# The dense activations' turned copies made in the forward chain instead of between the chains

## The chip, the cores and the metric

The kernel runs on one core of a Trainium2 chip. The metric is the device time of one execution in microseconds. A core has five engines with a queue of instructions each, executed in order: TensorE (PE) for matmuls, VectorE (DVE), ScalarE (ACT), GpSimd (POOL), and SyncE (SP), which here only issues transfers. Transfers run on 16 DMA engines that all queues share. PE reads its operands from on-chip memory (SBUF) and writes to accumulators (PSUM); the inputs, outputs and larger intermediates lie in DRAM.

## The reference

The kernel computes a forward pass and all its gradients. With `xn` the layer norm of `x` (2048 rows of 512), the output is `x + A(xn) + B(xn)`:

```python
# A: 64 segments of 32 rows, 8 memory rows carried from segment to segment
h = concatenate([mem, xs])                     # 40 x 512
q, k, v = h @ Wq, h @ Wk, h @ Wv               # 32 heads of 128
p = softmax(mask(q @ k.T * scale))             # 40 x 40 a head
o = (p @ v) @ Wo
mem, outs[s] = o[:8], o[8:]
# B
a = relu(xn @ w1 + b1) ** 2                    # 2048 x 1792
out = a @ w2 + b2
```

It returns the output and the gradients for `x`, the first memory, `Wq`, `Wk`, `Wv`, `Wo`, `w1`, `b1`, `w2` and `b2`, given `grad_out`, all in bfloat16. Two of them matter here: the gradient of `w2` is `a.T @ grad_out` and that of `w1` is `xn.T @ gh1`, where `gh1` is the gradient at `xn @ w1 + b1`. Both sum over all 2048 rows.

## The kernel before

The work runs in five stages, one after the other on PE. The times are those of the profiled execution.

1. **Dense part B** (0 to some 250 us): four blocks of 512 rows (`RB`). It makes `a` and `gh1` turned, with the 1792 features along the partitions, and stores them as `S_AT[rb]` and `S_GH1T[rb]` in DRAM (1792 x 512 each, rows of 1 KB).
2. **The forward chain** (some 250 to 1140 us): 64 steps, one for each segment, each waiting for the memory rows of the one before. Four steps make a block (`b`), and the memory rows of a whole block are computed apart in "left" work that runs some blocks behind or ahead.
3. **Between the chains** (some 1140 to 1377 us): 16 blocks of the first part of the backward pass for the memory rows (`lback`), and beside it, in the PE slots that `product` fills, the gradients of `w2` and `w1`.
4. **The backward chain** (some 1377 to 2340 us): 64 steps in the other direction.
5. **The weight gradients** of the attention (to the end at 2913 us).

**The order of work** in the stages 2 to 4 is written by hand. `F_ORDER` holds four strings, one for each step of a block; `play` (in the functions below) goes through them and calls each named operation. A plus or a minus behind a name shifts it to a later or an earlier step: `soP++` belongs to the step one before that of the names with three pluses. `L.` marks left work of a block. The calls issue instructions on all engines, and each engine's queue keeps the order of the calls. So the place of a name also decides where its transfer stands in SP's queue.

The names that matter, with the lines of the profile:

- `ld` (`load`, L639) loads 8 memory rows of v for a later step into `f_vLs`, four transfers of 16 KB. `w0` and `w1` read them on PE.
- `soV`, `soN`, `soP` (L956, L957, L958) store v, k with q, and the softmax `E` of a step to `S_A`. `E` is one tile, without a second buffer: the next step's `pm0` (DVE, L607) writes it again once the store has landed.
- `L.t0` to `L.t3` (L758) turn a quarter of a block's attention output by a DMA transpose of 256 KB into `OC`, a single buffer, and `L.u0` to `L.u3` (L766) store it.
- `L.lv` (L746), `L.lm` (L634) load `VL` and the four pieces of `vM`, 64 KB each; `L.W0` and `L.W1` on PE (L620, written as `f_pp<-ETL,vM`) read both.
- `kl` and `km` (L894, L895) are POOL's copies of the memory rows' keys into and out of `f_kT`; `kl` must be done before the step's scores.
- `L.hl`, `L.lq`, `L.ldL`, `L.lb` load further tiles, each well ahead of its use.

A transfer on SP also waits for the transfer eight places ahead of it in the same queue, since SP's transfers share eight semaphores in turn.

**Between the chains** `LB_ORDER` fixes the order of one block. Its `ld` (L1011 to L1014 and L629) loads the next block's `vTL` (a DMA transpose), `vTM`, `P`, `kM` in four pieces and `kL`, and then calls `chunk`. The gradient products go by 256 features at a time (`CH`), 7 for `w2` in the blocks 1 to 7 and 7 for `w1` in the blocks 9 to 15. For each, `chunk` brings one side into `wB` (two buffers of 1 MB, 128 partitions x 16 row blocks x 256 features, so that rows lie along the partitions): four DMA transposes of 256 x 512 on SP (L1085), one for each block of 512 rows. The other side (`wA`: `grad_out`, later `xn`, 2 MB) is loaded once by POOL (L1082). `product` multiplies half a piece at a time, 32 matmuls of 512 columns in a block (L1101, for `w2`) or 64 of 256 (L1106, for `w1`). A block of this stage on PE has in addition the projections by `Wo` (L422), the scores (L467) and the outer products (L620).

Two tiles of 128 KB, `XL0` and `X0`, hold the first left rows and the first block's input. They are made at the end of stage 1; `XL0` is read before the chain, `X0` by the first four steps and by a store to `S_HT`.

Of the kernel before, what the change touches and what calls it, by code (L numbers as in the profile page):

```python
# [10 lines left out]
BF16 = mybir.dt.bfloat16  # L11
F32 = mybir.dt.float32
P = 128
# [13 lines left out]
def kernel(  # L27
# [27 lines left out]
    nc = tc.nc  # L55
# [4 lines left out]
    F = B_w1.shape[1]  # L60
    SEG = int(A_seg_len)
    assert Dh == P and D % P == 0 and F % P == 0 and S % P == 0 and D <= 512
    L = M + SEG
    assert L <= 64 and P % SEG == 0
    NSEG = S // SEG
    DC = D // P
    TC = S // P
# [54 lines left out]
    S_GXNB = dram.tile([S, D], F32, name="S_GXNB")  # L122
    S_AT = dram.tile([NRB, F, RB], BF16, name="S_AT")
    S_GH1T = dram.tile([NRB, F, RB], BF16, name="S_GH1T")

    AC = 3 * GW + KH * KW
    S_A = dram.tile([NSEG, HG, SEG, AC], BF16, name="S_A")
# [526 lines left out]
    def play(order, n, steps, lefts, step, blk, done=None):  # L654
# [18 lines left out]
                            done(k)  # L673


    F_ORDER = (
# [3 lines left out]
        "ta+++ Ha+++ L.u2 L.mx0+ L.t1 soV+++ tb+++ L.X2 Hb+++",  # L680
# [5 lines left out]
        "rb+++ L.oa0+ ta+++ Ha+++ tb+++ Hb+++",  # L686
# [4 lines left out]
        "tu1+++ w1+++ L.lq++ oa1+++ ob1+++ g0+++ g1+++ soN++ ra+++ rb+++ ta+++ Ha+++ tb+++ L.otr+ Hb+++",  # L691
# [4 lines left out]
        "ta+++ Ha+++ rb+++ tb+++ Hb+++ km+++ L.t3+ q0mm++++ L.E5+ k0mm++++ L.ra+ xa+++ k0ev++++ q1mm++++ k1mm++++ "  # L696
        "q0ev++++ k0fl++++ q1ev++++ q0fl++++ k1ev++++ q1fl++++ xb+++ k0Te++++ soV++ kl++++ q1Te++++ k1fl++++ "
        "q0Te++++")
    ENGS = on_engines(
        "L.E1 L.E2 L.E4 L.oa0 L.ob0 k0ev k1ev oa0 ob0 ob1 q1Te q1ev ra rb v0ev v1ev",  # L700
        "L.E0 L.E3 L.E5 L.oa1 L.ob1 L.pm0 L.pm1 L.ra k0Te k1Te oa1 pm0 pm1 q0Te q0ev")
    with psum("fr", 4) as fr, psum("fpp", 1) as fpp, \
# [163 lines left out]
        def fwd(s):  # L866
# [84 lines left out]
            for h in range(2):  # L951
                o["H%s" % "ab"[h]] = lambda h=h: HTf(h)
                o["x%s" % "ab"[h]] = lambda h=h: half_over_groups(B_["XT"][:, 2 * h:2 * h + 2, j, M:SEG], st["T", h],
                                                                  slice(M, SEG))
            rows = S_A[s].rearrange("g r c -> (g r) c")
            o["soV"] = lambda: dma(rows[:, 0:GW], T["N"][:, 0, :])  # L956
            o["soN"] = lambda: dma(rows[:, GW:3 * GW], T["N"][:, 1:3, :].rearrange("p t c -> p (t c)"))  # L957
# [1 line left out]
            return o  # L959

        vLs = {}
        TURNS = [(Wqkv[t], n) for t in (1, 0, 2) for n in range(HD * DC // (8 * P))]
        TURNS_O = [(Wo, n) for n in range(HD * DC // (8 * P))]
        with tc.manual_schedule():
# [24 lines left out]
    with sb("la", 2) as la, sb("ls", 2) as ls, sb("lo", 1) as lo_, sb("wg", 2) as wg, psum("lpp", 1) as lpp, psum("lr", 4) as lr:  # L989
# [9 lines left out]
        def lback(i_):  # L999
            b = SEQ[i_]  # L1000
            shapes = {"vTM": [P, KH, HG, NL], "vTL": [P, KH, HG, NL], "P": [P, KH, KW], "kM": [P, GW], "kL": [P, GW],
                      "gON": [P, GW], "gOT": [P, KH, HG, NL],
                      "gS": [P, KH, KW], "gq": [P, KH, HG, NL]}
            home = {"gON": la, "gS": la, "gOT": lo_, "gq": lo_}
            T = Tiles(lambda n: home.get(n, ls).tile(shapes[n], BF16, name="l_" + n, tag=n, bufs=2))
            ps, st, o = {}, {}, {}

            def load(i1, q=nc.sync):
                T1, b1 = lb[i1][1], SEQ[i1]
                turned_rows(T1["vTL"][:], b1, 2)  # L1010
                q.dma_start(T1["vTM"][:], S_VTM[b1])  # L1011
                q.dma_start(T1["P"][:], S_PL[b1])
                memory_rows(T1["kM"], b1, 2 * GW, q)
                q.dma_start(T1["kL"][:], S_NL[b1][:, 1, :])  # L1014

            def ld():
                if i_ + 1 < NB:
                    load(i_ + 1)
                chunk(i_ + 1)
            o["ld"] = ld  # L1020
            o["first"] = lambda: (load(i_, nc.gpsimd), chunk(i_ + 1))
            for i in range(2):
                for x in range(2):
                    o["W%d%s" % (i, "ab"[x])] = lambda i=i, x=x: product(i_, i, x, ps)
                o["v%d" % i] = lambda i=i: keep(i_, i, ps)
                o["x%d" % i] = lambda i=i: store(i_, i, ps)
            for p in range(2):
                def mm(p=p):
                    ps["o", p] = big("ps_proj")
                    proj(ps["o", p], gol[:, :, b * NL:(b + 1) * NL], turned_columns(Wo), p)  # L1030
                o["o%dmm" % p] = mm
                o["o%dev" % p] = lambda p=p: acp(T["gON"][:, HC[p]], ps["o", p][:])

                def fl_(p=p):
                    ps["t", p] = tr("ps_tr")
                    flip(ps["t", p], T["gON"][:, HC[p]])
                o["o%dfl" % p] = fl_
                o["o%dte" % p] = lambda p=p: (acp, vcp)[p](T["gOT"][:, HALF[p]], kgr(ps["t", p]))

                def S_(p=p):  # L1040
                    ps["s", p] = big("ps_sc")
                    scores(ps["s", p], T["gOT"], ((T["vTM"], NL), (T["vTL"], NL)), p, None)
                o["s%d" % p] = S_
                ds_ops(o, p, KW, lambda p=p: ps["s", p], lambda: T["P"], lambda: T["gS"], lo_)

                def tu(p=p):
                    st[p] = ls.tile([P, 4, 2, 32], BF16, name="l_gST", tag="gST%d" % p)
                    turn(st[p], T["gS"], p)
                o["tu%d" % p] = tu

                def qp(p=p):
                    ps["x", p] = [lpp.tile([P, 2, 512], F32, name="l_pp", tag="pp%d" % x) for x in range(2)]
                    outer(ps["x", p], p, ((32, 32, False, 32, T["kM"], lambda k: st[p][:, k % 4, 0, :]),
                                          (32, 32, False, 32, T["kL"], lambda k: st[p][:, k % 4, 1, :])))
                o["qp%d" % p] = qp
                for x, n in enumerate("ab"):
                    o["qe%s%d" % (n, p)] = lambda p=p, x=x: acp(
                        T["gq"][:, HALF[p], 2 * x:2 * x + 2].rearrange("p k g r -> p g k r"), two_of(ps["x", p], x, 32))

            def so():  # L1060
                pdma(S_GOL[b], T["gON"][:])
                pdma(S_GSL[b], T["gS"][:])
                pdma(S_GQL[b], T["gq"][:])
            o["so"] = so
            return o, T
# [7 lines left out]
            n, second = (b - 1, False) if b <= NCH else (b - NCH - 2, True)  # L1073
            return (n if 0 <= n < NCH else None), second

        def chunk(b):
            n, second = job(b)
            if n is None or b in part:
                return
            if n == 0:  # L1080
                side[second] = wg.tile([P, TC, D], BF16, name="wA", tag="wA", bufs=1)
                pdma(side[second][:], (S_XN[:] if second else gflat).rearrange("(c p) f -> p c f", p=P))  # L1082
            part[b] = wg.tile([P, TC, CH], BF16, name="wB", tag="wB")
            for rb in range(NRB):
                nc.sync.dma_start_transpose(part[b][:, rb * RCB:(rb + 1) * RCB],  # L1085
                                            (S_GH1T if second else S_AT)[rb][n * CH:(n + 1) * CH, :])

        def turns(m):
            for x in range(min(m, len(TURNS))):
# [588 lines left out]
```

## Time and profile before

| | us |
|---|---|
| median of 3 timed runs | 2907.44 |
| their lowest and highest | 2903.41, 2910.01 |
| the profiled execution | 2915.0 |
| its span, first to last instruction | 2913.1 |

| engine | busy us | share | instructions |
|---|---|---|---|
| PE (matmul) | 2702.2 | 93% | 51252 |
| PEld (weight load) | 1450.9 | 50% | 51252 |
| DVE | 1277.8 | 44% | 3754 |
| ACT | 1001.7 | 34% | 2330 |
| POOL | 660.6 | 23% | 1278 |

SP has no busy time in this table, since issuing a transfer is not counted; the order of time of its queue shows how long each issue took. The DMA engines moved 561.50 MB, 193 GB/s over the span; 642177 of the 835429 packets were under 512 B.

How to read the lines: a group names source line, engine, operation, output and inputs, then partitions x elements, count and times. "Idle before" is the time in which that engine did nothing ahead of the group's instructions, with what ended it. A line of stretches gives the window and its length, the busy time of PE, PEld, DVE, ACT and POOL with the number of instructions, the granted TensorE clock as a share of full speed, the busy share of the 16 DMA engines (overlapping packets can bring it above 1), and GB/s. A line of an engine's time order gives start, length, engine, line, operation and how many were merged. Waits are listed as total us, number and longest.

### The profile page before, as it was taken

To read this page: it belongs to the slowest core of one execution; us is meant where nothing else is said; L and a number is where in the kernel's file an instruction comes from. 1 tells how busy PE (TensorE), PEld (TensorE's weight loads), DVE (VectorE), ACT (ScalarE), POOL (GpSimd) and SP (SyncE) were. 2 spreads that over 40 slices of the span, in tenths; PEclk is the share of its full clock that TensorE was granted. 3 is DMA by queue.
4 is the path that set the end of the run, shared out by engine and by line. 5 is a ranking of instruction groups with operands and counts; after the bars stand their busy time and mean duration, and the time that the engine had idled before them with its cause. 6 is when DMAs were issued, how large, how long until landed. Compare 5 with 4: busy or idle time off the path is not lost.

```text
span 2913.1 us, 115280 instructions
## 1 busy us (share of the span) xinstructions
PE 2702.2 (93%) x51252; PEld 1450.9 (50%) x51252; DVE 1277.8 (44%) x3754; ACT 1001.7 (34%) x2330; POOL 660.6 (23%) x1278
## 2 busy tenths in 40 slices
PE   7997999999999887888898999999999999999999
PEld 3444555555555555355454554455555444444444
DVE  4533566666665654343454545454445401100000
ACT  2313444444444445232333333333333301111111
POOL 1000000000000001122333433343334324332221
PEclk9998999999999998998899999999999999999999
DMA  9766477667676668999666687677767799999993
GB/s 250 259 207 164 138 184 189 184 188 182 180 192 166 170 156 201 227 225 213 148 167 164 179 220 173 172 180 211 184 170 181 223 273 224 220 209 237 217 210 71
DMA packets 835429, 561.50 MB, mean 193 GB/s; under 512 B 642177, under 2 KB 727698, under 8 KB 833394
## 3 DMA queue, kind: packets, MB, share of 16 engines
q1 hardware_dynamic: 794018, 431.40, 64.6%
q0 software_dynamic: 40912, 122.73, 14.0%
q8 instruction: 402, 6.59, 0.9%
q14 instruction: 97, 0.79, 0.1%
HBM read 174.47 MB, written 234.11 MB: 140 GB/s over the span
## 4 chain that ended last, share of the span: by engine, by line
PE 42%; DMA 7%; issue 2%; DVE 1%; SPq 1%; POOL 0%; ACT 0%; ACTq 0%; DVEq 0%; POOLq 0%
PE ps_gw L1639 17%; PE ps_gR L490 11%; PE ps_proj L422 3%; PE b_pp L620 3%; PE ps_RL L1251 3%; DMA b_kLs<-S_NL 2%; PE b_T L525 1%; PE ps_tr L164 1%; DMA gn<-S_OL 1%; DMA b_qN<-S_A 1%; PE ps_R L490 1%; DMA S_GM<-b_GN 1%; PE b_pp L1383 1%; PE ps_sc L467 1%; DMA b_GN<-GT 0%
## 5 line engine op out<-in xcount | busy, mean ns | idle before, releaser
L1639 PE MATMUL ps_gw<-gn,HNc 128*128 128x512 bf16 x1920 | 416.8, 379 | 0.0
L1639 PEld LDWEIGHTS <-HNc 128*128 128x128 bf16 x1920 | 187.9, 98 | 223.6
L404 ACT CAST f_N<-ps_proj 128x512 bf16<-128x512 f32 x320 | 183.9, 581 | 199.4 <-PE ps_proj L422 192.6
L1572 ACT CAST wt<-ps_gw 128x512 bf16<-128x512 f32 x128 | 74.0, 588 | 451.3 <-PE ps_gw L1639 412.0
L422 PEld LDWEIGHTS <-X 128*32 128x32 bf16 x6144 | 152.6, 96 | 143.1 <-DVE X L534 21.9
L1555 DVE TENSOR_TENSOR gx<-ps_rows,gb 128x512 f32<-128x512 f32 x16 | 11.1, 692 | 426.4 <-PE ps_rows L1553 426.4
L895 POOL COPY kM<-f_kT 128x256 bf16<-128x256 bf16 x64 | 25.8, 403 | 736.0 <-DVE f_kT L407 562.2
L490 PE MATMUL ps_gR<-Wv,gv 128*32 128x512 bf16 x2048 | 145.0, 404 | 6.9 <-issue 6.9
L1639 PE MATMUL ps_gw<-GOc,gn 128*128 128x512 bf16 x640 | 141.0, 383 | 10.2 <-ACT wt L1572 8.7
L490 PE MATMUL ps_gR<-Wk,gk 128*32 128x512 bf16 (+1 forms) x2048 | 141.1, 387 | 1.3 <-ACT gk L404 0.8
L490 PE MATMUL ps_R<-Wo,OT 128*32 128x256 bf16 x4096 | 135.6, 289 | 1.1 <-DVE OT L407 1.1
L422 PE MATMUL ps_proj<-Wq,X 128*32 128x512 bf16 x2048 | 134.7, 380 | 0.1
L404 ACT CAST gk<-b_pp 128x256 bf16<-128x256 f32 x192 | 70.7, 379 | 184.0 <-PE b_pp L620 116.1
L422 PE MATMUL ps_proj<-Wk,X 128*32 128x512 bf16 x2048 | 130.9, 380 | 0.8
L422 PE MATMUL ps_proj<-Wv,X 128*32 128x512 bf16 x2048 | 131.3, 382 | 0.0
L404 ACT CAST gON<-ps_proj 128x512 bf16<-128x512 f32 x128 | 75.0, 586 | 157.4 <-PE ps_proj L422 157.4
L490 PE MATMUL ps_gR<-Wq,gq 128*32 128x512 bf16 (+1 forms) x2048 | 122.8, 348 | 6.8 <-issue 6.8
L422 PE MATMUL ps_proj<-Wo,GT 128*32 128x512 bf16 x2048 | 123.3, 382 | 3.7 <-DVE GT L1296 3.6
L1573 POOL DMA_DIRECT2D out_dram<-wt x120 | 65.0, 543 | 255.7 <-ACT wt L1572 241.0
L1332 POOL COPY PD<-b_P 32x320 bf16<-32x320 bf16 x256 | 115.3, 450 | 8.0
L490 PEld LDWEIGHTS <-OT 128*32 128x32 bf16 x4096 | 109.3, 102 | 9.9 <-DVE OT L407 1.3
L1327 POOL DMA_DIRECT2D b_P<-S_A x63 | 33.9, 538 | 349.9 <-DVE gS L579 115.6
(276 smaller groups left out, 5256.7 us busy)
## 6 DMA issues: line engine op xcount, KB each, us to landing
S_A<-f_N SPq DMA_DIRECT2D x64, 512.0 KB
out_dram<-wt POOLq DMA_DIRECT2D x134, 128.0 KB, 4.9
S_A<-f_N SPq DMA_DIRECT2D x64, 256.0 KB
S_GB<-gv SPq DMA_DIRECT2D x32, 512.0 KB
S_GB<-gq SPq DMA_DIRECT2D x32, 512.0 KB
S_GB<-gk SPq DMA_DIRECT2D x32, 512.0 KB
b_kN<-S_A POOLq DMA_DIRECT2D x63, 256.0 KB, 3.9
b_qN<-S_A POOLq DMA_DIRECT2D x63, 256.0 KB, 4.1
```

Of the source, the lines that this page charges most:

```text
L164: nc.tensor.transpose(ps_ap, in_ap, ident[base:base + k, base:base + k])
L404: nc.scalar.copy(out, in_)
L422: nc.tensor.matmul(o, lhsT=hT[:, dc, :], rhs=x, start=(dc == 0), stop=(dc == DC - 1), tile_position=(0, 32 * g))
L467: nc.tensor.matmul(sc3[32 * g:32 * g + 32, k, c:c + n], lhsT=qT[:, 4 * h + k, g, :], rhs=kT[:, 4 * h + k, g, :], start=(mask is None), sto ...
L490: nc.tensor.matmul(R[32 * g:32 * g + 32, 0:(cs.stop - cs.start) * P].rearrange("p (a b) -> p a b", b=P), lhsT=XT(k, g), rhs=x[:, cs, :], s ...
L620: nc.tensor.matmul(o, lhsT=N_[32 * g:32 * g + m, kk * P:(kk + 1) * P], rhs=X(kk)[32 * g:32 * g + m], start=(i == 0), stop=(i == len(jobs) ...
L1251: nc.tensor.matmul(ps["R", i][32 * g:32 * g + 32, :].rearrange("p (a b) -> p a b", b=P), lhsT=B_[n][:, k, g, :], rhs=W(g * KH + k), start= ...
L1327: q(tile_of("P", [P, KH, KW])[:], rows[:, 3 * GW:AC].rearrange("p (k n) -> p k n", k=KH))
L1332: nc.gpsimd.tensor_copy(PD[32 * g:32 * g + 32, g], C["P"][32 * g:32 * g + 32, :, 0:L])
L1572: nc.scalar.copy(wt[:], ps[:])
L1573: eng(dst, wt[:])
L1639: nc.tensor.matmul(ps[:], lhsT=l(rc), rhs=r(rc), start=(n == 0), stop=(n == RC_ALL - 1))
```

## The change

In the forward chain, two operations a step and box are added: `aw0` and `aw1` turn one unit of 256 features x 256 rows (128 KB) from `S_AT` or `S_GH1T` into a box by a DMA transpose on SP, and `as0` and `as1` store the box from POOL to its place in `S_AN` or `S_GH1N`, two new DRAM tensors in which a piece of 1 MB lies as `wB` wants it. The boxes are `XL0` and `X0`, which are free by then. The 112 units belong to the steps 3 to 58. Between the chains, `chunk` loads its piece with one plain transfer of 1 MB, on SP and the very first on POOL.

```diff
+    S_AN = dram.tile([F // (2 * P), P, TC, 2 * P], BF16, name="S_AN")
+    S_GH1N = dram.tile([F // (2 * P), P, TC, 2 * P], BF16, name="S_GH1N")
...
+            for i in range(2):
+                u = UNITS.get((s, i))
+                o["aw%d" % i] = lambda i=i, u=u: nc.sync.dma_start_transpose(
+                    BOX[i], u[0][u[3]][u[2] * 2 * P:(u[2] + 1) * 2 * P, u[4] * 2 * P:(u[4] + 1) * 2 * P]) if u else None
+                o["as%d" % i] = lambda i=i, u=u: pdma(
+                    u[1][u[2]][:, u[3] * RCB + 2 * u[4]:u[3] * RCB + 2 * u[4] + 2, :], BOX[i]) if u else None
...
+        BOX = [x[:].rearrange("p c r -> p (c r)").rearrange("p (a f) -> p a f", f=2 * P) for x in (XL0, X0)]
+        units = [(a, b, n, rb, hf) for a, b in ((S_AT, S_AN), (S_GH1T, S_GH1N)) for n in range(F // (2 * P))
+                 for rb in range(NRB) for hf in range(2)]
+        assert RCB == 4 and 2 * U0 + len(units) <= 2 * NSEG
+        UNITS = {(U0 + x // 2, x % 2): u for x, u in enumerate(units)}
...
-            o["first"] = lambda: (load(i_, nc.gpsimd), chunk(i_ + 1))
+            o["first"] = lambda: (load(i_, nc.gpsimd), chunk(i_ + 1, pdma))
...
-        def chunk(b):
+        def chunk(b, eng=dma):
...
-            for rb in range(NRB):
-                nc.sync.dma_start_transpose(part[b][:, rb * RCB:(rb + 1) * RCB],
-                                            (S_GH1T if second else S_AT)[rb][n * CH:(n + 1) * CH, :])
+            eng(part[b][:], (S_GH1N if second else S_AN)[n])
```

`F_ORDER` gets the new names; the four strings are also cut at other places, and where names pass such a cut their shift changes by one. A few names trade places with a neighbour (`L.lq` with `ob1`, `rb` with `ta`). The new order around the places that the prediction speaks of:

```diff
+        "k1mm++++ soP+++ L.sb1+ aw0+ k0ev++++ xa+++ q1mm++++ k1ev++++ q1ev++++ L.ex0+",
+        "L.lv+ q0fl+++ xb++ L.u1 k0fl+++ k1fl+++ q1fl+++ q0Te+++ k0Te+++ soN++ s0+++ v0mm+++ k1Te+++ mx0+++ q1Te+++ "
+        "as1- sb0+++ s1+++ ex0+++ su0+++ km+++ mx1+++ rc0+++ v1mm+++ sb1+++ L.P0+ ld++ v0ev+++ pm0+++ aw1 ex1+++ "
+        "tu0+++ su1+++ rc1+++ w0+++ v1ev+++ pm1+++ ob0+++ L.t0 L.lm+ L.P1+ tu1+++ w1+++ L.su0+ oa0+++ ld++++ L.ex1+ "
+        "L.rc0+ g0+++ oa1+++ L.pm0+ L.su1+ L.tu0+ ob1+++ g1+++ L.W0+ L.BT ld+++ ra+++ L.E0+ as0 L.oa0+ ta+++ rb+++ "
+        "Ha+++ tb+++ Hb+++ k0mm++++ L.ob0+ L.u0 L.rc1+ q0mm++++ L.E1+ k1mm++++ aw0+ L.out xa+++ q1mm++++ L.pm1+",
...
+        "q1fl+++ k1Te+++ L.oa1+ s0+++ mx0+++ as1- q1Te+++ L.hs+ sb0+++ L.X0+ aw1 v0mm+++ soP++ L.ob1+ s1+++ ex0+++ "
```

More of the change, by code (lines that the diff above doesn't have):

```diff
@@ L673, in play @@
                             done(k)
+    U0 = 3
     F_ORDER = (
[3 rows of a table removed]
-        "ta+++ Ha+++ L.u2 L.mx0+ L.t1 soV+++ tb+++ L.X2 Hb+++",
[5 rows of a table removed]
-        "rb+++ L.oa0+ ta+++ Ha+++ tb+++ Hb+++",
[4 rows of a table removed]
-        "tu1+++ w1+++ L.lq++ oa1+++ ob1+++ g0+++ g1+++ soN++ ra+++ rb+++ ta+++ Ha+++ tb+++ L.otr+ Hb+++",
[4 rows of a table removed]
-        "ta+++ Ha+++ rb+++ tb+++ Hb+++ km+++ L.t3+ q0mm++++ L.E5+ k0mm++++ L.ra+ xa+++ k0ev++++ q1mm++++ k1mm++++ "
-        "q0ev++++ k0fl++++ q1ev++++ q0fl++++ k1ev++++ q1fl++++ xb+++ k0Te++++ soV++ kl++++ q1Te++++ k1fl++++ "
-        "q0Te++++")
[19 rows of a table added]
+        "oa1+++ g1+++ ra+++ ta+++ Ha+++ rb+++ tb+++ aw0 Hb+++ km+++ L.t3+ q0mm++++ L.E5+ k0mm++++ L.ra+ xa+++ "
+        "k0ev++++ q1mm++++ k1mm++++ q0ev++++ k0fl++++ q1ev++++ q0fl++++ aw1 k1ev++++ q1fl++++ xb+++ k0Te++++ soV++ "
+        "kl++++ as0 q1Te++++ k1fl++++ q0Te++++")
     ENGS = on_engines(
```

28 rows, old and new, of the table F_ORDER are left out of this document.

## The prediction

> **What bounds the kernel now.** I read the page's slices first, then the busy time by stage, then who made PE wait, then the order of SP's queue. By the slices PE is busy for nearly the whole span, so only stages with idle PE can give time back. The stretches below show PE's busy us first, then PEld, DVE, ACT and POOL, and at the end the granted clock, the DMA share and GB/s.
>
> ```profile
> 350.00:880.00 530.00, 520.70 (x13088) 296.26 (x13091) 344.16 (x1074) 257.79 (x591) 32.22 (x80) 1.00 0.71 185
> 1168.70:1241.70 73.00, 58.56 (x1001) 26.06 (x1000) 27.38 (x64) 17.71 (x40) 13.47 (x25) 0.95 1.07 230
> 1287.30:1357.90 70.60, 59.77 (x1165) 43.40 (x1167) 27.30 (x64) 17.71 (x40) 18.77 (x35) 0.93 1.09 232
> 1329.80:1340.80 11.00, 11.00 (x233) 8.35 (x232) 3.83 (x10) 3.54 (x8) 3.75 (x7) 0.98 1.06 225
> 1205.00:1207.40 2.40, 0.05 (x2) 0.04 (x2) 0.00 (x0) 0.00 (x0) 0.64 (x2) 1.00 1.34 150
> 1207.40:1210.80 3.40, 3.40 (x71) 1.41 (x72) 1.05 (x3) 0.00 (x0) 0.00 (x0) 0.50 1.10 302
> ```
>
> The forward chain (first line) has PE at 98% with the DMA engines at 0.71. The stage between the chains (next two: five blocks each) has PE at 80 to 85% and the DMA engines at over 1.0. One of its blocks (fourth line) ran with PE busy for all of its 11.0 us; the ten blocks of both lines took (73.0 + 70.6) / 10 = 14.4 us each. What ended PE's idle time there:
>
> ```profile
> PE ps_w L1101 <- DMA wB<-S_AT: 14.7, 13, 2.5
> PE ps_w L1106 <- DMA wB<-S_GH1T: 12.2, 12, 2.3
> ```
>
> Total us, times, longest: PE waits for the turned pieces, 27 us in all. Why they are late stands in SP's queue, one block of that stage (start, us):
>
> ```profile
> 1221.06 1.51 SPq L629 DMA_TRANSPOSE l_vTL<-S_NL  x1
> 1222.62 0.60 SPq L1011 DMA_DIRECT2D l_vTM<-S_VTM  x1
> 1223.32 0.39 SPq L1012 DMA_DIRECT2D l_P<-S_PL  x1
> 1223.80 3.61 SPq L634 DMA_DIRECT2D l_kM<-S_A  x4
> 1227.52 0.41 SPq L1014 DMA_DIRECT2D l_kL<-S_NL  x1
> 1228.03 8.22 SPq L1085 DMA_TRANSPOSE wB<-S_AT  x4
> ```
>
> There is no gap: SP issues from end to end, 8.2 of some 15 us for the four transposes, and the DMA engines are full. PE's own work is 11 us. So DMA work and its issue bound this stage, PE the forward chain.
>
> **The change, part by part.** PE's and DVE's instructions stand in the same order in both programs; on ACT one copy (R from ps_R, 0.37 us) stands one place later in each block. What moves is SP and POOL.
>
> *Taken from the stage between.* 56 transposes of 256 KB leave, 14 plain loads of 1 MB come (one by POOL). The issue falls from 8.2 to about 0.6 us (a plain issue in the fence is 0.4 to 0.6), so SP needs 7 of 11 us. In DMA time: in 1169 to 1256 the hardware queue had 35502 packets in 86.8% of 16 engines, 34 ns each, and 32640 of them were under 512 B; a 1 MB piece in 256 B packets is 4096, or at most 4096 x 34 / 16 = 8.7 us of all engines. A plain load goes by the software queue's row of that stretch (5.63 MB in 18.5% of 87 us x 16 = 257 engine-us, 22 KB each): 3.0 us. Total: 1.06 x 14.5 - 8.7 + 3.0 = 9.7 us a block, below PE's 11.0, but not by much, and the 1 MB is issued last of nine. I take 11.6 us a block, near the gapless block's row. Ten blocks: 143.6 - 116 = **27.6 us saved**. Ends: 11.0 (PE alone) saves 33.6; 12.4 (halfway to today's 14.4, give or take) saves 20. For the three blocks between (1241.7 to 1287.3, 45.6 us with PE busy 37.5) I add 3.5 us: SP stood 16.7 us at one set of four transposes beside the 2 MB load of the second left side, but the stores behind that load stay late. Ends 0 and 6. Stage: **-31**, from -20 to -39.
>
> Part of that is clock. The last two lines of the first fence show PE idle for 2.35 of 2.4 us, and then 3.4 us at 0.50 of the clock; PE's 58.56 busy us in five blocks are 11.7 each, not 11.0. The Trainium skill (TensorE: Matmul & The Clock Gate, HAM oscillation) says that PE should have no idle gaps above some 3.4 us. Taken as a threshold it speaks against a gain in clock here, since the longest wait for wB is 2.5 us; the blocks would then need 11.8 us busy ((58.56 + 59.77) / 10) and the ten would save 25. The trace shows the half rate behind the shorter gap, so the sum keeps 27.6.
>
> *Added to the forward chain on SP.* 112 transposes of 128 KB over 56 steps, two a step. No such transpose from DRAM is in the trace; nearest is b_GN<-GT, 128 KB from SBUF, median 1263 ns, and the 256 KB ones there (OC<-OT) take 1269; under load wB's median is 1750. I take 1.26 + 0.06 gap: 10.6 us for a block of four steps, 53 us. SP waits today in 615 to 668 for 15.6 of 53 us, so there is room on average, but not everywhere:
>
> ```profile
> 625.02 0.43 SPq L746 DMA_DIRECT2D VL<-S_NL  x1
> 625.55 0.41 SPq L766 DMA_DIRECT2D S_ON<-OC  x1
> 626.01 0.42 SPq L957 DMA_DIRECT2D S_A<-f_N  x1
> 626.48 1.95 SPq L639 DMA_DIRECT2D f_vLs<-S_NL  x4
> 629.01 1.27 SPq L758 DMA_TRANSPOSE OC<-OT  x1
> 630.32 2.82 SPq L634 DMA_DIRECT2D vM<-S_A  x4
> ```
>
> In PE's order the first matmul that reads this vM:
>
> ```profile
> 638.24 0.20 PE L620 MATMUL f_pp<-ETL,vM 32*128 32x32 bf16 x4
> ```
>
> Now aw0 stands ahead of VL, aw1 ahead of OC: 2 x 1.32 us against one gap of 0.58. vM comes 2.1 us later here, up to 2.6 where the gap is missing. Its last issue began about 632.4, 5.8 us ahead of its reader; 3.7 are left. SP's landings are not in the page; POOL's rows are 3.0 us for 32 KB (PGD), 4.6 for 64 KB (l_kM). And vM already ends waits of PE in four places between 350 and 900 (1.3 us). So a block loses 0 to 2.6 us; behind PE's in-order queue nothing else fills it. I take 0.9: 14 blocks x 0.9 = **+12**.
>
> The second place is soP, the store of E. SP goes without a gap from 637.93 to it at 640.98; aw0 and aw1 stand between, +2.6 us, so 643.6. The next write of E (DVE L607, at 647.26) must wait for it to land: 3.7 us left against 3.3 to 4.8 for 128 KB on POOL's rows (b_P, S_GSL). 0 to 1.2 us a block; I take 0.3: **+4**. f_vLs is issued at least 4.5 us ahead of its reader and comes 1.3 later: inside the 3.0 us of PGD's row, nothing. X, kL, qL, VL, dN and f_N have 7 to 40 us: nothing.
>
> *Added on POOL.* 112 stores of 0.54 us (the row of its DMA issues). POOL works 3.2 us in 53. Each store waits for its transpose (some 3 to 5 us) and kM and kL's copy queue behind it; kM waits for DVE or PE 10.8 to 12.4 us in each step anyway, so nothing; without that cover s0 would be late by what the transpose lacks, perhaps 2 us. Each aw waits for the store of its box a step before: 5 + 0.5 + 5 = 10.5 of 13.2 us, nothing, but close.
>
> *DMA engines in the forward chain.* 2.1 MB more a block (8 units in and out). At the hardware queue's rate in 350 to 880 (96.07 MB in 69.7% of 530 us x 16, 16 KB per engine-us) that is 8 us of 53: the share goes from 0.71 to 0.86. Landings lengthen; I put that into the bounds.
>
> **Sum.** -31 + 12 + 4 = -15, against the profiled execution's 2915.0 us (span 2913.1 and 1.9 around it): 2900. That execution is 7.6 us above the median of the timed runs, 2907.4; 15 below that is **2892**. Forward cost by its ends: 0 to 14 x (2.6 + 1.2) = 53, of which I hold half likely at most.
>
> **The rivals.**
> 1. *The forward chain hides it all.* For: SP waits for 15.6 us a block, the tight places miss by less than a landing varies, and a late chain gives SP time back. Against: vM had no room in four places before. Forward cost 0 to 5, stage -31 to -35: 2875.
> 2. *SP becomes the bound of the forward chain (slower).* Place: vM and soP in each block. From about 2.3 us of idle PE a half-rate window follows (the row at 1205), 1.7 us more. If SP's issue under a fuller DMA queue takes 1.75 us (wB's median), two transposes cost 3.6 instead of 2.6; vM then misses by 2 to 2.5 and soP by 1, with the half rate in most blocks: 14 x (2.2 + 1 + 1) = 59 less some 14 that SP wins back. +45 - 31: 2921. It decides from 31 / 14 = 2.2 us a block.
> 3. *The stage between stays at the DMA engines.* 2.1 MB a block must still come in one burst behind PE's release of the buffers; if the 1 MB lands late each time the blocks stay at 13.2 us: -12, with +16 before it: 2911. For: shares over 1.0 now. Against: the small packets are what fills them.
>
> **How the numbers follow.** Forecast 0.42 (2883 to 2902), rival 1 0.22, rival 2 0.20, rival 3 0.16. About 0.2%, 5.8 us, is what a measurement of this kernel can tell from no change. Faster by more: the forecast (0.40) and rival 1 (0.22): 0.62. Within: the rest of the forecast and most of rival 3: 0.15. Slower: rival 2 and a little of 3: 0.23. The range from 2868 (stage -39, forward nothing) to 2918 leaves out the upper part of rival 2 and little else, some 0.17.
>
> **What would show it.** Right: no wait for wB left, blocks of 11 to 12 us with granted clock near 1.0 and DMA share below 1; in the forward chain waits of PE for vM of around 1 us a block, of DVE's E for S_A<-E of less, and the chain 10 to 20 us longer. Wrong: blocks above 12.4 us (DMA still bounds), waits for f_vLs or kL (SP's order is worse than the fence shows), 0.50 clock inside 310 to 900, or an SP issue of the 128 KB transposes far from 1.26 us.

## The result and the profile after

The change made the kernel slower: 2980.05 us median of four runs (2973.16 to 2994.0) beside 2907.26 for the kernel before (2903.41 to 2910.01), a ratio of 1.0244 (95% interval 1.0211 to 1.0276). The prediction had 2892, from 2868 to 2918. The profiled execution took 2974.32 us (span 2972.5), 59.3 more than that of the kernel before; the three stages below add up to 59.9, while the medians lie 72.8 apart.

By stage (the forward chain from its first step's `exp` on ACT, the stage between from its first `o0mm` on PE, the backward chain from its first `o0mm` to its last):

| stage | before, us | after, us | difference | forecast |
|---|---|---|---|---|
| forward chain | 882.5 | 973.5 | +91.0 | +16 |
| between the chains | 233.7 | 204.9 | -28.8 | -31 |
| backward chain | 934.6 | 932.3 | -2.3 | 0 |

Between the chains the time came out close to the forecast. The same stretches after the change (columns as in the prediction's first fence; the forward chain, five blocks for `w2`, five for `w1`, one block):

```profile
350.00:880.00 530.00, 478.51 (x11436) 271.07 (x11475) 302.46 (x944) 226.02 (x521) 66.31 (x140) 0.95 0.80 196
1261.30:1316.30 55.00, 52.37 (x986) 26.12 (x1000) 25.87 (x61) 17.71 (x40) 13.45 (x25) 1.00 1.10 286
1363.20:1419.70 56.50, 54.50 (x1161) 41.69 (x1160) 27.10 (x64) 17.67 (x40) 18.75 (x35) 1.00 1.02 275
1272.00:1283.50 11.50, 10.52 (x202) 5.32 (x208) 5.52 (x14) 3.54 (x8) 2.69 (x5) 1.00 1.07 283
```

PE's waits for `wB` went from 27 us to one:

```profile
PE ps_w L1113 <- DMA wB<-S_AN: 0.5, 1, 0.5
```

The ten blocks take 55.0 + 56.5 = 111.5 us in place of 143.6, 11.2 each, with the clock at 1.00. The DMA share stayed above 1.0, but now PE sets the pace.

The loss is in the first line: PE busy for 90% of the stretch where it was 98, and a clock of 0.95 where it was 1.00. From PE's matmul records and the clock windows over the whole chain, PE's idle time went from 46.4 to 107.5 us (+61.1), and the time lost to the half clock (one minus the granted share, summed) from 21.0 to 52.8 (+31.8). The rest, PE's work at full clock, is the same within 2 us. By steps, some four fifths of the loss lie in one step of each block, the first: 18.7 us on average in place of 13.8. Some waits in 350 to 1100 us and what ended them (total us, times, longest), after and before:

```profile
PE f_pp L622 <- DMA f_vLs<-S_NL: 20.4, 15, 3.5
PE f_pp L622 <- ACT OT L406: 22.5, 15, 3.3
ACT OT L406 <- DMA OC<-OT: 16.6, 4, 5.1
DVE E L609 <- DMA S_A<-E: 8.7, 5, 2.3
PE f_pp L622 <- DMA vM<-S_A: 2.9, 6, 1.0
```

```profile
PE f_pp L620 <- ACT OT L404: 2.5, 5, 0.5
ACT OT L404 <- DMA OC<-OT: 1.1, 1, 1.1
PE f_pp L620 <- DMA vM<-S_A: 0.6, 2, 0.3
```

`vM`, on which most of the forecast loss was put, is the smallest of these. The large ones had no price in the prediction: `f_vLs`, put at nothing (PE had no such wait before), and ACT's write of `OT`, which must wait until `L.t0` (L761) has read that buffer out; PE then waits for ACT. SP's queue in one block shows both late. The `exp` of this block's first step starts at 610.7; in the block that the prediction shows, at 632.6.

```profile
592.67 1.24 SPq L761 DMA_TRANSPOSE OC<-OT  x1
594.00 0.53 SPq L965 DMA_DIRECT2D S_A<-f_N  x1
594.58 1.29 SPq L776 DMA_TRANSPOSE vTM<-vM  x1
595.97 1.24 SPq L960 DMA_TRANSPOSE X<-S_AT  x1
597.26 0.58 SPq L846 DMA_DIRECT2D S_PL<-EL  x1
597.89 0.78 SPq L966 DMA_DIRECT2D S_A<-f_N  x1
598.77 0.39 SPq L769 DMA_DIRECT2D S_ON<-OC  x1
602.92 1.24 SPq L761 DMA_TRANSPOSE OC<-OT  x1
...
609.44 2.36 SPq L641 DMA_DIRECT2D f_vLs<-S_NL  x4
611.90 1.39 SPq L960 DMA_TRANSPOSE X<-S_AT  x1
613.38 1.25 SPq L761 DMA_TRANSPOSE OC<-OT  x1
```

`f_vLs` was issued 6.1 us ahead of the `exp` (626.48 against 632.6) and now 1.3; `L.t0` 3.6 ahead and now 2.7 behind. The gap from 599.2 to 602.9 looks like room, but it is SP waiting for its own store of `OC` to land, since `OC` is one buffer: turn, store, turn, store, four times a block. Whatever delays one store delays every turn behind it. SP's waits for these stores kept their length: 2.2 us each before (32 of them) and after (26).

What follows on PE in the next us: it idles 1.46 us for `f_vLs` from 613.55 and 1.07 us for ACT's `OT` from 616.57. The granted clock falls to half at 616.8, inside the second gap, and stays there until 623.6:

```profile
613.50:617.60 4.10, 1.54 (x31) 0.73 (x31) 0.87 (x3) 0.66 (x3) 0.54 (x1) 0.90 0.86 135
617.60:621.00 3.40, 3.36 (x92) 2.62 (x95) 2.01 (x5) 0.84 (x3) 0.00 (x0) 0.50 0.33 109
```

### The profile page after: what moved, and what is told of

It is laid out like the page before. It is cut to its first block, busy times and chain, and to the rows that moved or that the text cites. A ratio compares the mean times of both kernels' runs of the same rounds, so it can differ in the third digit from the quotient of the medians.

```text
span 2972.5 us, 115524 instructions
## 1 busy us (share of the span) xinstructions
PE 2724.4 (92%) x51115; PEld 1466.2 (49%) x51252; DVE 1277.2 (43%) x3754; ACT 1001.1 (34%) x2330; POOL 720.5 (24%) x1391
## 4 chain that ended last, share of the span: by engine, by line
PE 71%; DMA 14%; SPq 6%; DVE 3%; issue 3%; ACT 2%; POOL 0%; ACTq 0%; DVEq 0%; POOLq 0%
PE ps_gw L1651 15%; PE ps_proj L424 13%; PE ps_gR L492 11%; PE ps_R L492 4%; DMA b_kLs<-S_NL 3%; PE b_pp L622 3%; PE ps_RL L1263 3%; PE ps_tr L166 2%; PE ps_L L382 2%; PE ps_w L1118 2%; PE ps_B L343 2%; PE ps_gxb L352 2%; PE ps_sc L469 1%; PE f_pp L622 1%; PE f_T L527 1%
## 5 line engine op out<-in xcount | busy, mean ns | idle before, releaser
L406 ACT CAST f_N<-ps_proj 128x512 bf16<-128x512 f32 x320 | 183.8, 581 | 206.0 <-PE ps_proj L424 190.4
L492 PE MATMUL ps_R<-Wo,OT 128*32 128x256 bf16 x4096 | 149.9, 309 | 1.1 <-DVE OT L409 1.1
L492 PEld LDWEIGHTS <-OT 128*32 128x32 bf16 x4096 | 116.1, 109 | 16.9 <-DVE OT L409 1.3
```

The lines of the kernel that those rows point to most:

```text
L406: nc.scalar.copy(out, in_)
L492: nc.tensor.matmul(R[32 * g:32 * g + 32, 0:(cs.stop - cs.start) * P].rearrange("p (a b) -> p a b", b=P), lhsT=XT(k, g), rhs=x[:, cs, :], s ...
```

## The experiments

Three theories. **A**: SP's queue; the issue of the transposes and the chain of SP's waits for its own transfers make `f_vLs`, `L.t0` and `E` late. **B**: the fuller DMA engines make every transfer land later. **C**: POOL's stores and their waits. A fourth, **D**, came up on the way: the full-sized transposes in SP's queue cost by themselves.

All numbers in one table, in us. Chain, idle and clock are as above; "L.t0" is the start of that turn against the `exp` of the block's first step (median of 11 blocks, plus is late). The last column is the whole and, in brackets, the kernel before on the same chip. Where the text gives no interval, the whole is one execution. Two executions of the untouched forward chain gave 882.5 and 880.5, so the chain is the surer number; the time from the stage between to the first weight gradient, which no edit touches, varies from 949 to 973 us over these 20 executions.

| run | chain | PE idle | clock | L.t0 | between | whole |
|---|---|---|---|---|---|---|
| before | 882.5 | 46.4 | 21.0 | -3.5 | 233.7 | |
| the change | 973.5 | 107.5 | 52.8 | +3.0 | 204.9 | |
| stage between alone | 880.5 | 46.2 | 18.6 | -3.5 | 205.3 | 2883.9 (2923.1) |
| tiny turns | 924.3 | 82.4 | 23.1 | +0.7 | 206.0 | 2920.7 (2895.5) |
| POOL loads, no turns | 891.1 | 58.9 | 13.4 | -3.0 | 210.2 | 2888.9 (2895.5) |
| both halves | 957.5 | 94.4 | 44.8 | +2.1 | 207.9 | 2969.5 (2923.1) |
| order | 973.6 | 111.4 | 51.5 | +0.1 | 209.9 | 2983.9 (2895.5) |
| half the units | 923.8 | 69.7 | 34.6 | +0.4 | 226.0 | 2945.5 (2923.1) |
| half, other places | 914.2 | 72.4 | 19.9 | -1.2 | 223.7 | 2935.1 (2914.0) |
| loads by POOL | 1012.0 | 126.0 | 77.2 | +1.7 | 203.3 | 3016.7 (2895.5) |
| stores by POOL | 970.4 | 111.8 | 49.4 | +2.9 | 208.2 | 2982.1 (2923.1) |
| small loads by POOL | 955.0 | 100.1 | 46.5 | +0.1 | 217.4 | 2993.8 (2914.0) |
| the same, and order | 953.6 | 99.2 | 38.9 | -2.4 | 215.6 | 2977.1 (2914.0) |
| small loads, no units | 892.0 | 60.9 | 14.9 | -5.2 | 242.1 | 2926.3 (2913.9) |
| small loads, no stores | 929.0 | 86.4 | 28.2 | -1.2 | 220.5 | 2940.2 (2913.9) |
| larger units | 910.0 | 69.3 | 21.2 | -0.8 | 207.3 | 2917.3 (2913.9) |
| larger units, POOL loads | 928.8 | 83.8 | 26.4 | -0.7 | 214.2 | 2927.1 (2913.9) |
| larger units, chain first | 893.6 | 58.8 | 16.3 | -2.4 | 204.6 | 2903.4 (2911.1) |
| the same, vM by POOL | 900.6 | 67.8 | 14.7 | -2.3 | 207.0 | 2918.2 (2911.1) |
| before, chain first | 882.6 | 47.3 | 22.9 | -4.1 | 233.8 | 2907.6 (2910.8) |

### The two halves of the change apart

*The stage between alone:* the kernel before, with one plain load a piece.

```diff
-            for rb in range(NRB):
-                nc.sync.dma_start_transpose(part[b][:, rb * RCB:(rb + 1) * RCB],
-                                            (S_GH1T if second else S_AT)[rb][n * CH:(n + 1) * CH, :])
+            eng(part[b][:], (S_GH1T if second else S_AT).rearrange("b f r -> (b f r)").rearrange(
+                "(n p c x) -> n p c x", p=P, c=TC, x=CH)[n])
```

> The kernel before, with its forward chain untouched; between the chains each piece comes in one plain load of 1 MB of unturned data, so the gradients of w1 and w2 are not computed. If the two halves of the change are separate: the forward chain stays at 882 us and the stage between at 205 (233.7 before), the whole about 29 under the kernel before. If the late start or the POOL load of the first piece plays a part: 207 to 212.

The chain stayed at 880.5, the stage took 205.3. The halves are separate, and the whole question is the forward chain.

### SP's issue or the bytes

*Tiny turns:* the instruction stays on SP, the bytes go.

```diff
-                    BOX[i], u[0][u[3]][u[2] * 2 * P:(u[2] + 1) * 2 * P, u[4] * 2 * P:(u[4] + 1) * 2 * P]) if u else None
+                    BOX[i][:, 0, 0:32], u[0][u[3]][u[2] * 2 * P:u[2] * 2 * P + 32, u[4] * 2 * P:u[4] * 2 * P + P]) if u else None
```

> The changed kernel, with each of the 112 transposes cut from 256 x 256 to 32 x 128 (8 KB), and no box stored; the chunks between the chains are plain loads of unturned data, so the gradients of w1 and w2 are not computed. SP's queue keeps its instructions in their places, the DMA engines lose some 27 MB of transposes and stores. Theory A (SP's queue: the issue of the transposes, and the chain of waits in it, makes f_vLs and the turns of OT late once a block): the forward chain, 882.5 us before and 973.5 after, stays at 955 to 980, if a small transpose is issued in the same 1.2 to 1.3 us; the whole about 2960 to 2980. Theory B (the fuller DMA engines make every transfer land later): the chain falls back to 885 to 900, the whole about 2885 to 2895.

*POOL loads, no turns:* the bytes stay, SP is free.

```diff
-                o["aw%d" % i] = lambda i=i, u=u: nc.sync.dma_start_transpose(
+                o["aw%d" % i] = lambda i=i, u=u: [pdma(
+                    BOX[i].rearrange("p a (b c) -> p b a c", b=2)[:, :, a],
...
+                        "p (b c) -> p b c", b=2)) for a in range(2)] if u else None
```

> The changed kernel, with each 128 KB transpose on SP replaced by two plain loads of 64 KB on POOL in 256 byte pieces; the store of the box stays. Nothing is turned, so the gradients of w1 and w2 are not computed. SP is as free as before the change, the DMA engines carry the same bytes in packets of the same size. Theory A: the forward chain is back at 882 to 895 us (973.5 with the change), the whole about 2880 to 2895. Theory B: it stays at 950 to 975, the whole at 2950 to 2975. A third theory, C (POOL's stores and its waits make kM and kL late): also 950 to 975, but then POOL's copies kL and kM are what PE waits for.

Here B and C fall as the cause. The same stretch of the run with POOL loads, and of the change:

```profile
350.00:1100.00 750.00, 706.46 (x18058) 408.88 (x18100) 469.78 (x1479) 352.13 (x811) 217.21 (x438) 0.99 0.82 214
```

```profile
350.00:1100.00 750.00, 670.78 (x16277) 384.36 (x16322) 427.73 (x1341) 318.96 (x736) 94.64 (x200) 0.95 0.81 196
```

The order of work is that of the change, the DMA share is as high (0.82 and 0.81), and the median landing of `OC`, `S_ON`, `f_vLs` and `vM` is even longer than with the change (3.6, 4.1, 3.4 and 3.9 us from start to landed, against 3.3, 3.3, 3.2 and 3.6), but the chain costs 9 us, not 91. SP's issue alone (the tiny turns) cost 42, though, not the 73 to 98 expected of A. Of this PE's idle time is 36 and the clock only 2.

*Both halves:* a tiny turn on SP and the loads on POOL in each place.

> The two experiments that each kept one half, put together: a tiny transpose (16 x 128) on SP in each of the 112 places, and beside it the bytes by two plain loads on POOL with the store of the box. Nothing is turned rightly, so the gradients of w1 and w2 are not computed. Apart, SP's issue cost 42 us in the forward chain and the bytes 9. Theory A+B (the same slack is spent by both: SP's issue makes transfers late, and the longer landings then count in full): the chain at 950 to 975 us, the whole at 2950 to 2975. Theory D (the two add up, and the rest, some 40 us, belongs to the full-sized transposes in SP's own queue): the chain at 930 to 940 us, the whole at 2925 to 2940.

957.5: +75, where 42 + 9 are 51, as theory A+B forecast. So the two don't add up, they spend the same slack. How is argued, not shown: SP's issue takes the slack, then each longer landing counts (the turn of `OT` landed in 3.9 us here, in 3.5 with the tiny turns), and the gaps come close enough for the half clock (+24 where each half alone had +2 and -8). With the change itself that turn landed in 3.3 us (3.4 before), so longer landings of this chain are not what it lost by. What the full transposes have beyond the 75 is 16 us.

### Order, number and place

*Order:* `f_vLs` (`ld`) ahead of `aw0`, `aw0` to behind the store of `OC`, `aw1` behind `L.t0`, `vM` and the next `f_vLs`.

```diff
-        "k1mm++++ soP+++ L.sb1+ aw0+ k0ev++++ xa+++ q1mm++++ k1ev++++ q1ev++++ L.ex0+",
+        "k1mm++++ soP+++ ld+++ L.sb1+ k0ev++++ xa+++ q1mm++++ k1ev++++ q1ev++++ L.ex0+",
...
-        "as1- sb0+++ s1+++ ex0+++ su0+++ km+++ mx1+++ rc0+++ v1mm+++ sb1+++ L.P0+ ld++ v0ev+++ pm0+++ aw1 ex1+++ "
+        "as1- sb0+++ s1+++ ex0+++ su0+++ km+++ mx1+++ rc0+++ v1mm+++ sb1+++ L.P0+ aw0 v0ev+++ pm0+++ ex1+++ "
```

> The changed kernel, complete; only the places in SP's order move: the load of f_vLs for the block's first step goes ahead of aw0 (some 3 us earlier), aw0 goes behind VL and the store of OC into the gap in which the next turn waits for that store, and aw1 goes behind the turn L.t0, vM and the next f_vLs. Same issue time, same DMA work. Theory A in its narrow form (those two transposes ahead of f_vLs and L.t0 are the cost): the forward chain falls from 973.5 to 885 to 915 us, the whole to 2885 to 2920. Theory A in its wide form (SP is simply full, whatever the order): the loss moves to other transfers and the chain stays at 940 to 975, 2940 to 2980. Theory B: no change, 2960 to 2980.

The wide form of A: nothing gained. PE's 20.4 us of waits for `f_vLs` are gone, and the loss is elsewhere, more than half of it in the block's second step (16.1 us; 13.9 with the change, 12.8 before), where the write of `E` now waits:

```profile
DVE E L609 <- DMA S_A<-E: 27.4, 12, 4.1
ACT OT L406 <- DMA OC<-OT: 18.4, 5, 4.3
```

*Half the units:* `aw0` and `as0` alone, for `w2`.

```diff
+        UNITS = {(U0 + x, 0): u for x, u in enumerate(units)}
```

> The changed kernel, complete, with one unit a step (aw0 and as0 of the steps 3 to 58) for the gradient of w2 alone; the pieces of w1 are turned between the chains as before. SP gets 5.3 us more a block in place of 10.6. If SP's queue has room for a part (theory A with a slack): the forward chain costs 10 to 30 us in place of 91, the stage between gains 14 to 17; the whole 2890 to 2910. If the cost goes with each transpose in SP's queue (theory D): half of 91, the chain at 925 to 930, the whole at 2935 to 2945.

*Half, other places:* the same 56 units with both boxes in the third and fourth step.

```diff
+        UNITS = {(6 + x // 4 * 4 + x % 4 // 2, x % 2): u for x, u in enumerate(units)}
```

> The same 56 units as in the run with half the units, complete, but in other places: both boxes in the third and fourth step of each block, none in the first two, in which the chain of turns and stores of OT (L.t3 to L.t0, each waiting for the store before it) and the load of f_vLs stand. Same number of transposes and bytes. Theory A with a place (only what stands ahead of that chain in SP's queue costs): the forward chain falls from 924 to 883 to 895 us (882.5 before). Theory D (each transpose costs wherever it stands): it stays at 915 to 930.

Both missed A's forecast and came within 1.2 us of D's range. Half the units cost 41 us, nearly half of 91, so there was no free part; away from the chain of turns they still cost 32. SP's delay reaches `L.t0` from there too (-1.2 where it was -3.5), and more of the loss now lies in the block's second step (13.9 us; 12.8 before) than in the first (14.6; 13.8).

### Taking other work off SP

*Loads by POOL* (`f_vLs`, `vM`), *stores by POOL* (`soV`, `soN`, `soP`, `L.u0` to `L.u3`) and *small loads by POOL* (`f_vLs`, `vM`, `VL`, `X`, `bb`, each where its buffer is free) are edits of one kind:

```diff
-                left_of_step(dma, t[:], b1, j1, 2)
+                left_of_step(pdma, t[:], b1, j1, 2)
```

> The changed kernel, complete, with the loads of f_vLs (16 a block) and vM (4 a block) issued by POOL in place of SP. That takes some 11 us of issue a block off SP, about what the transposes put on (10.6), and takes f_vLs and vM out of SP's order. DMA traffic as in the changed kernel, POOL has more. Theory A: the forward chain comes to 885 to 905 us (973.5 with the change), the whole to 2880 to 2905. Theory B: no change of the chain beyond 10 us, 2960 to 2980. Theory C: as bad or worse, over 2970, since POOL's queue has 20 more transfers a block.

> The changed kernel, complete, with SP's stores of each step (v, k with q, E) and of OC issued by POOL, behind whose waits no load stands: SP loses 16 issues of some 0.47 us a block, 7.5 of the 10.6 us added, and no longer waits in its queue for OC to land ahead of its store. DMA traffic as in the changed kernel. Theory A (SP's queue is the cost): the forward chain 885 to 920 us, the whole 2880 to 2920. Theory D (full-sized transposes in SP's queue cost by themselves): 930 to 960, the whole 2925 to 2955. If POOL's own waits hold the stores up, E's above all: worse than 973.

> The changed kernel, complete, all 112 units in their places; POOL issues f_vLs, vM, VL, X and bb, 23 transfers and some 13 us of issue a block, more than the 10.6 added to SP. Against the earlier run with loads by POOL each load stands where its buffer is free, between POOL's copy kL and the next kM, and the store of the box ahead of it. Theory A: the forward chain 885 to 910 us (973.5 with the change), no waits of PE for f_vLs; the whole 2880 to 2905. If POOL's waits for DVE and PE hold its loads up: 940 to 1000.

All missed A's forecast: 1012, 970 and 955. POOL executes in order too, and its own waits hold the transfers up: with the stores by POOL it stood 155 us in 750 until turns of `OT` had landed, and SP waited for a box some 87; with the loads by POOL, PE waited 40.6 us for `f_vLs`. *The same, and order* puts `L.u2` ahead of `aw1` and `aw1` behind `L.t0`:

> As the run with the small loads by POOL, and in SP's order the chain of turns goes first: the store of OC (L.u2) is issued as soon as the turn has landed, ahead of aw1, and aw1 of the block's second step stands behind L.t0. Theory A with a place: the forward chain 880 to 895 us, the whole 2870 to 2890, ACT's wait of OT for OC gone. If order counts for little once SP has room: as the other run, within 8 us.

`L.t0` came at -2.4 and ACT's wait for `OC` fell to 5.1 us, but the chain stayed at 953.6. SP still waited 91 us for boxes, and the loss now lies in the first step (15.9 us; 13.8 before) and in the fourth (15.4; 13.2 before).

Two more runs separate what POOL does: *small loads, no units* is the kernel before with those loads by POOL; *small loads, no stores* drops the `as` from the run with the small loads by POOL.

> The kernel before, complete and without any unit, with the small loads by POOL (f_vLs, vM, VL, X, bb, in the places of the run with the small loads by POOL). Control for that run. If POOL issues them in time: the forward chain within 8 us of 882.5, the whole within 10 us of the kernel before. If POOL's waits make them late by themselves: 910 to 960, and the loss of that run is POOL's, not the transposes'.

> The run with the small loads by POOL, without the stores of the boxes; the chunks are plain loads of unturned data, so the gradients of w1 and w2 are not computed. SP's transposes no longer wait for a box. If SP's waits for the boxes (63 us in 750) were what kept that run at 955 us: the forward chain 885 to 905. If the transposes cost by themselves even where SP has fewer issues than before the change: 930 to 955.

Neither gave its first case: 892.0 and 929.0. POOL's loads alone cost 10 us of the chain (and 8 between); the boxes' stores, with SP's waits for them, were 26 of the 73 us; the other 37 came with the transposes, although SP issued no longer than before the change (505 of 750 us; 509 before). In that run the median turn of `OT` took 4.5 us to land (3.4 before, 3.7 with the loads by POOL and no units), four of them in the chain.

### Fewer, larger turns, and the chain of turns first

*Larger units:* one box of 256 KB and 56 units of 256 x 512, at the places where SP waits for `OC`.

```diff
+                BX = smp.tile([P, 2, DC, P], BF16, name="BX")
+                XL0, X0 = BX[:, 0], BX[:, 1]
...
+            o["aw"] = lambda: nc.sync.dma_start_transpose(
+                BOX, u[0][u[3]][u[2] * 2 * P:(u[2] + 1) * 2 * P, :]) if u else None
+            o["as"] = lambda: pdma(u[1][u[2]][:, u[3] * RCB:(u[3] + 1) * RCB, :], BOX) if u else None
```

> Complete; the two boxes become one of 256 KB, and 56 units of 256 x 512 are turned, one a step, in the places in which SP waited for the store of OC or had a gap (behind L.u3, L.u2, L.u0 and L.ldL); all loads by SP as in the changed kernel. An issue costs about the same for 256 KB as for 128 KB (1.27 and 1.26 us), so SP gets 5.1 us more a block with all of the gain between the chains. Theory A: the forward chain at 895 to 920 us, the whole 2890 to 2915. If it is the bytes turned through SP's queue and not the issues: 950 to 975, the whole over 2940.

All bytes, half the issues, other places: +27.5 us in place of +91. D by bytes falls; D by the number of transposes does not, and this run cannot tell number from place. *Larger units, POOL loads* adds the small loads by POOL:

> As the run with larger units, and the small loads by POOL. SP has then some 8 us of issue a block less than before the change. Theory A: the forward chain 882 to 900 us, the stage between 205 to 210, the whole 2875 to 2895. If POOL's queue is what fails: no better than the larger units alone.

Worse by 19 us, and SP had gaps: the chain of turns ran on landings alone (4.2 us a turn, 4.2 a store, 3.4 and 3.3 before), so `L.t0` was no earlier. That would be B's part. What is left is when the stores of the chain are issued. *Chain first* moves three names:

```diff
-        "L.hl++ k1Te+++ L.lb s0+++ mx0+++ sb0+++ L.X1 L.ta s1+++ L.u3 aw v0mm+++ mx1+++ ex0+++ soP++ su0+++ "
+        "L.u3 L.hl++ k1Te+++ L.lb s0+++ mx0+++ sb0+++ L.X1 L.ta s1+++ aw v0mm+++ mx1+++ ex0+++ soP++ su0+++ "
...
-        "L.lv+ q0fl+++ xb++ L.u1 k0fl+++ k1fl+++ q1fl+++ q0Te+++ k0Te+++ soN++ s0+++ v0mm+++ k1Te+++ mx0+++ q1Te+++ "
+        "L.u1 L.lv+ q0fl+++ xb++ k0fl+++ k1fl+++ q1fl+++ q0Te+++ k0Te+++ soN++ s0+++ v0mm+++ k1Te+++ mx0+++ q1Te+++ "
```

(and `L.u2` from behind `Ha+++` to ahead of `L.lp`).

> As the run with larger units, complete; in SP's order the stores of OC go first: L.u3 ahead of the loads of X and bb, L.u2 ahead of the store of EL, L.u1 ahead of VL, so that each is issued when its turn has landed (1.7, 1.1 and 0.6 us earlier in the block read). Nothing else moves. If the lateness of L.t0 is what costs (median 3.5 us ahead of the step's exp before the change, 3.0 behind it with the change, 0.8 ahead with larger units): L.t0 comes 2 to 3.5 us earlier and the forward chain falls from 910 to 890 to 900 us; the whole 8 to 20 us under the kernel before. If L.t0 is only a sign: 905 to 915, the whole within 5 us of the kernel before.

`L.t0` came 1.6 us earlier, a little less than expected, and the chain fell by 16.4 us to 893.6. Nothing but three stores in SP's order had moved, so the lateness of the chain that they belong to is shown as a cause, not only as a sign; each side is one profiled execution. Its stretch, and SP's queue ahead of an `exp` at 584.1:

```profile
350.00:1100.00 750.00, 708.98 (x17987) 408.21 (x18020) 471.53 (x1480) 351.89 (x809) 74.85 (x167) 0.99 0.90 216
```

```profile
576.21 0.73 SPq L770 DMA_DIRECT2D S_ON<-OC  x1
577.00 0.45 SPq L750 DMA_DIRECT2D VL<-S_NL  x1
577.49 0.88 SPq L965 DMA_DIRECT2D S_A<-f_N  x1
578.47 1.93 SPq L642 DMA_DIRECT2D f_vLs<-S_NL  x4
580.50 1.82 SPq L762 DMA_TRANSPOSE OC<-OT  x1
```

`f_vLs` is 5.6 us ahead again and `L.t0` 3.6, with the DMA share at 0.90. The whole is a little faster than the kernel before: ratio 0.9969 (0.9946 to 0.9993), 2903.4 beside 2911.1, just short of the 8 us expected. That is less than the two stages suggest (-29 + 11). The profile is of the fastest of its twelve executions, 2884.81, which also spent 12 us less than the kernel before behind the stage between, so the chain of the others may be longer. *The same, vM by POOL:*

> As the run with larger units and the chain of turns first, and vM's four loads by POOL, which takes 2.8 us off SP right behind L.t0 (PE waited for vM 7 us in 750 with larger units). If vM was late by SP: the forward chain 3 to 8 us shorter than the other run of this call, the whole 10 to 25 us under the kernel before. If POOL's queue is no better: the same or a few us longer.

A miss: ratio 1.0009 (0.9984 to 1.0035), the chain 7 us longer. *Before, chain first*, the control:

> The kernel before, complete and without any unit, with the stores of OC in the places of the run with larger units and the chain of turns first (L.u3, L.u2, L.u1 ahead of loads and other stores). Control for that run: if the order helps only where SP is full, the forward chain stays at 880 to 885 us and the whole within 4 us of the kernel before, since L.t0 is in time there already. If the order is worth something by itself, the chain falls below 878 and the gain of that run is not the units' alone.

Ratio 1.0000 (0.9971 to 1.0028), the chain 882.6: the order was worth something only where SP had the transposes to issue as well.

## Why the prediction was wrong

- **Stage between, -31: right.** Measured -28.8. The ten blocks saved 32.1 (27.6 forecast; the clock was 1.00 where it had been 0.95 and 0.93), the three around the second left side lost 1.3 where 3.5 were to be saved, and the first and last blocks lost 2. The share below 1 that was to show it did not come; rival 3's price did not either.
- **Issue of a transpose, 1.26 us: right** as a median (1.25), with a mean of 1.42.
- **"SP waits today in 615 to 668 for 15.6 of 53 us, so there is room on average": the step that failed.** It counted all waits alike. SP issued for 509 of 750 us before and 611 after, so it was never full, and yet its last link, `L.t0`, came 6.5 us later. SP's waits show why: those for DVE's `E` were room and were used up, those for its own store of `OC` stayed. Before, then after:

```profile
SPq L758 <- DMA S_ON<-OC: 70.1, 32, 4.8
SPq L958 <- DVE E L607: 45.5, 27, 5.3
```

```profile
SPq L761 <- DMA S_ON<-OC: 57.7, 26, 4.2
SPq L967 <- DVE E L609: 2.9, 4, 1.2
```

  The second kind are links of the chain turn, store, turn; they move with the delay. Even 56 transposes of 128 KB found no free room in the two sets of places tried (+41 and +32).
- **`f_vLs`, "at least 4.5 us ahead of its reader and comes 1.3 later", nothing: wrong** by the same step. Only the transpose right ahead of it was counted; the delay of what stands ahead in the block adds up, and it came some 5 us later (6.2 us ahead of the `exp` before, 1.2 after, medians of 11 blocks). PE waited 20.4 us for it in 750.
- **`vM`, +12, and `soP` with `E`, +4: wrong places.** PE waited 2.9 us for `vM` and DVE 8.7 for `E` in 750. `L.t0` had no term at all, nor ACT's wait for it (16.6) or PE's for ACT (22.5, 2.5 before).
- **The half clock** was in rival 2, not in the sum: +31.8 of 91. The Trainium skill (TensorE: Matmul & The Clock Gate, HAM oscillation and A second HAM failure mode) gives two cases, idle gaps above some 3.4 us and short pauses between groups of matmuls that come often. The prediction weighed the first; the trace is nearer to the second: in the block shown half rate set in after gaps of 1.46 and 0.25 us. Rival 2's "about 2.3 us" came from one row; in the forward chain of the kernel before, half rate had already followed 1.54 us of idle time in 3.41.
- **POOL, nothing; DMA engines in the bounds: right** as far as they go. 9 us with the same bytes off SP; but where SP is late as well, the bytes cost more (75, not 51).
- **Rival 2** had the mechanism (SP becomes the bound, the half rate follows) at half the price (+45 in the chain) and in the wrong places, with a chance of 0.20.

Not settled: how the last 16 us of the 91 divide between SP's waits for the boxes (6 us in 750) and the size of the transposes, and why the bytes cost 33 us where SP is late and 9 where it isn't.

## What to carry to other kernels

A queue's waits are room only if what it waits for comes from elsewhere; waits for its own transfers, through a single buffer, are a chain that shifts as a whole. Before adding to such a queue, follow the chain to its last link and compare that with its reader: here 3.5 us of lead were enough and 2.4 nearly, as long as nothing else came late. Then add few, large transfers, behind the links of the chain and not ahead of them: that cost 11 us in place of 91.

## What the runs showed of the hardware

- A DMA transpose held SP's queue 1.1 to 1.25 us (minimum) whether it moved 4, 8, 128 or 256 KB: medians of 1.2, 1.2, 1.25 and 1.3 us (with both halves, tiny turns, the change and larger units, in 350 to 1100 us; between the chains before, with the DMA share over 1.0, the median was 1.75). So in the chain SP's issue goes by the number of transposes. The same 14.7 MB in 56 turns cost the chain 27.5 us, in 112 turns 91, but the places differ too.
- The half clock came from short idle pieces that lie close together. In these traces the granted clock holds for whole multiples of 3.41 us. Cut at those edges, the forward chain with the change goes from full to half rate 21 times, 20 of them right behind 3.41 us in which PE was idle for 1.54 us or more (by its matmul records); no such stretch at full rate with over 1.73 us of idle time was followed by full rate. In the block shown it was 1.78 us idle, in pieces of at most 1.46, and then 6.8 us at 0.50.
- Between the chains PE ran at full clock and almost without waits for its pieces with the DMA share at 1.02 to 1.10.
